# The first loads of a fused attention and MLP kernel: x's second tile on ACT's queue, b1 first on GpSimd's queue, b1's transpose behind those of the normalised rows

## The chip, the core and the metric

One NeuronCore of a Trainium2 chip runs the whole kernel. Its engines work side by side and meet through semaphores: PE (TensorE, the matrix unit, with its weight loads listed apart as PEld), DVE (VectorE), ACT (ScalarE), POOL (GpSimd) and SP (SyncE, here only an issuer of DMAs). SP, ACT and POOL each have a DMA queue of their own; in the profile these are q1 (SP), q10 (ACT) and q0 (POOL, called software_dynamic). An engine takes its instructions in the order in which they are written, and an instruction that waits holds up all behind it on that engine.

The metric is the device time of one launch in microseconds (us). The kernel before takes 795.08 us, the median of three runs (794.21 to 796.0).

## What is computed

Input x has 2048 rows of 512. Part A is a recurrent attention: the rows are cut into 64 segments of 32, each segment attends over 8 memory rows and itself with 32 heads of 128, and the first 8 output rows become the memory of the next segment. Part B is an MLP on every row. A gate mixes both:

```python
def _B_ref(x, w1, b1, w2, b2):
    y = _layernorm(x, axis=-1)
    h = _gelu(jnp.einsum('bsd,df->bsf', y, w1) + b1)      # 512 -> 1376
    return jnp.einsum('bsf,fd->bsd', h, w2) + b2          # 1376 -> 512
...
g = _sigmoid((x * gate_w).sum(-1, keepdims=True))
a = _A_ref(x, A_mem0, A_Wq, A_Wk, A_Wv, A_Wo, A_seg_len)
b = _B_ref(x, B_w1, B_b1, B_w2, B_b2)
return g * a + (1 - g) * b
```

All inputs are bf16.

## The kernel before, in words

The MLP runs first, over all rows, and leaves (1 − g) b in a DRAM buffer `c_dr`; meanwhile the attention's large weights come in. Then the 64 segments run one after another. The order on each engine is the order of the program text (a manual schedule). The change touches only the start, the part before and around the first MLP block.

The MLP works on 8 blocks of two tiles of 128 rows. For each block, `prep` normalises: per tile `bn_stats` and `bn_aggr` on DVE (L422, L423), then for both tiles together the inverse root (for block 0 a square root on ACT, L426, and a reciprocal on DVE), then the normalised rows `y` (L434). `prep_tr` turns a tile of y by four PE transposes (L441; each is a matmul with the identity) into the PSUM banks X1 or X2 and copies the result on DVE to `yT` (L442). `a_mm` multiplies one of 11 slices of 128 columns of w1 with yT, four matmuls of 256 columns (L462), alternately into the PSUM banks SbF and W, and ACT applies gelu with the bias `b1_sb` (L463) into `hTm`. `b_mm` multiplies hTm with w2, two matmuls of 512 columns (L468), two units behind `a_mm`. So the first three units of `a_mm` stand alone, and from then on units of both alternate.

The bias b1 has 1376 values and has to stand across partitions, one column of 128 for each slice. It is loaded as 11 rows of 128 into `b1r` (two DMAs, since the last row has only 96 values; a memset fills the rest), turned by one PE transpose into `b1p`, which lies in bank W (L498), and copied to `b1_sb` by DVE (L500).

The order before the first block is this. POOL: the memsets of `BO`, the making of the identity `ident`, the memset of b1r (L324), the load of the gate weights `gw_bc` (L336, a broadcast to 128 partitions), constants for the masks. SP's queue: x's tiles 0 and 1 (`ld_x`, L309), the first 3 of 11 slices of w1 (L322), b1's two pieces (L325, L326), x's tiles 2 and 3, w1's slices 3 to 6 (L334) and 7 to 10 (L335), the later part of w2 (L337, L338), b2, x's tiles 4 and 5. ACT's queue: w2's slices 0 to 2 and 3 to 5 (L331), then a first activation that loads ACT's table. PE: 28 warm-up matmuls on the identity (L496, into bank U3, their results unused), the transpose of b1, the eight transposes of y, then `a_mm` of block 0. DVE: `prep(0)`, the copy of b1, the two copies of yT, then `prep(1)`.

The lines that order this on PE and DVE:

```python
        for _ in range(NWARM):
            nc.tensor.matmul(U[3][:, 0:P], lhsT=ident[:], rhs=ident[:], start=True, stop=True, skip_group_check=True)
        b1p = W[:].bitcast(BF16)[:, 0:FC]
        nc.tensor.transpose(b1p, b1r[:], ident[:FC, :FC])
        prep(0)
        nc.vector.tensor_copy(out=b1_sb[:], in_=b1p)
        for tt in range(TB):
            prep_tr(0, tt)
```

Of the kernel before, what the change touches and what calls it, by code (L numbers as in the profile page):

```python
# [10 lines left out]
BF16 = mybir.dt.bfloat16  # L11
# [16 lines left out]
def kernel(ctx, tc, A_x, A_mem0, A_Wq, A_Wk, A_Wv, A_Wo, A_seg_len, B_x, B_w1, B_b1, B_w2, B_b2, gate_w, out):  # L28
    nc = tc.nc
    P = 128  # L30
# [6 lines left out]
    F = B_w1.shape[1]  # L37
# [3 lines left out]
    FC = (F + P - 1) // P  # L41
# [11 lines left out]
    x2 = A_x.rearrange("b s d -> (b s) d")  # L53
# [8 lines left out]
    ident = pers.tile([P, P], BF16)  # L62
# [6 lines left out]
    ep = early.enter_context(tc.tile_pool(name="ep", bufs=1))  # L69
# [9 lines left out]
    SelL = ep.tile([P, P], BF16)  # L79
    SelI = ep.tile([P, 32], BF16)  # L80

    nc.gpsimd.memset(BO[:], 0.0)
    for g in range(4):
        nc.gpsimd.memset(BO[32 * g:32 * g + 32, 32 * g:32 * g + 32], 1.0)
# [207 lines left out]
    with tc.tile_pool(name="mlpw", bufs=1) as mlpw, \  # L292
# [2 lines left out]
        TB = 2  # L295
        NBLK = NT // TB
        LAG = 2
        FR = F - (FC - 1) * P
        assert FR % 32 == 0 and FR < P
        w1_sb = mlpw.tile([P, KC, F], BF16)  # L300
        w2_sb = mlpw.tile([P, FC, Dm], BF16)
        b1_sb = mlpw.tile([P, FC], BF16)
# [1 line left out]
        hTm = [mlpw.tile([P, FC, TB * P], BF16, name=f"hTm{i}") for i in range(2)]  # L304
        xts = {}

        def ld_x(T):
            xt = mwork.tile([P, Dm], BF16, tag="xt", bufs=6, name="xt")
            nc.sync.dma_start(xt[:], x2[T * P:(T + 1) * P, :])  # L309
            xts[T] = xt  # L310

        def ld_w(W_, A, n):
# [4 lines left out]

        F0 = 3 * P
        ld_x(0)
        ld_x(1)  # L320
        w1v = B_w1.rearrange("(kc p) f -> p kc f", p=P)
        nc.sync.dma_start(w1_sb[:, :, 0:F0], w1v[:, :, 0:F0])  # L322
        b1r = mlpw.tile([FC, P], BF16)
        nc.gpsimd.memset(b1r[:], 0.0)  # L324
        nc.sync.dma_start(b1r[0:FC - 1, :], B_b1[0:(FC - 1) * P].rearrange("(c p) -> c p", p=P))  # L325
        nc.sync.dma_start(b1r[FC - 1:FC, 0:FR], B_b1[(FC - 1) * P:F].rearrange("(o p) -> o p", o=1))  # L326

        NWARM = 28
        H1, H2, F1 = 3, 6, 7 * P
        for a, b in ((0, H1), (H1, H2)):  # L330
            nc.scalar.dma_start(w2_sb[:, a:b, :], B_w2[a * P:b * P, :].rearrange("(fc p) d -> p fc d", p=P))  # L331
        ld_x(2)
        ld_x(3)
        nc.sync.dma_start(w1_sb[:, :, F0:F1], w1v[:, :, F0:F1])  # L334
        nc.sync.dma_start(w1_sb[:, :, F1:F], w1v[:, :, F1:F])  # L335
        nc.gpsimd.dma_start(gw_bc[:], gate_w.partition_broadcast(P))  # L336
        nc.sync.dma_start(w2_sb[:, H2:FC - 1, :], B_w2[H2 * P:(FC - 1) * P, :].rearrange("(fc p) d -> p fc d", p=P))  # L337
        nc.sync.dma_start(w2_sb[:FR, FC - 1, :], B_w2[(FC - 1) * P:F, :])  # L338
        nc.sync.dma_start(w2_sb[FR:FR + 1, FC - 1, :], B_b2.rearrange("(o d) -> o d", o=1))
        ld_x(4)  # L340
# [40 lines left out]
        def consts():  # L381
            nc.vector.tensor_scalar(out=rr[:, 0:1], in0=ri[:], scalar1=31, scalar2=None, op0=ALU.bitwise_and)
            nc.vector.tensor_scalar(out=rr[:, 2:3], in0=rr[:, 0:1], scalar1=2, scalar2=None, op0=ALU.logical_shift_right)
            nc.vector.tensor_scalar(out=rr[:, 1:2], in0=rr[:, 0:1], scalar1=3, scalar2=None, op0=ALU.bitwise_and)
            nc.vector.tensor_copy(out=rf[:], in_=rr[:])
            nc.vector.tensor_copy(out=iof[:], in_=io[:])
            nc.vector.tensor_scalar(out=rf[:, 0:1], in0=rf[:, 0:1], scalar1=float(M), scalar2=None, op0=ALU.subtract)
            nc.vector.tensor_scalar(out=mk1[:], in0=iof[:, 0:4], scalar1=rf[:, 1:2], scalar2=MASK_NEG, op0=ALU.not_equal, op1=ALU.mult)
            yield
            for a in range(4):  # L390
                nc.vector.tensor_scalar(out=Mk[:, a, 16:16 + RIDE], in0=iof[:], scalar1=rf[:, 0:1], scalar2=MASK_NEG, op0=ALU.is_lt, op1=ALU.mult)
                nc.vector.tensor_copy(out=Mk[:, a, 0:8], in_=mk1[:, a:a + 1].to_broadcast([P, 8]))
                nc.vector.tensor_scalar(out=Mk[:, a, 48:56], in0=iof[:, 0:8], scalar1=rf[:, 2:3], scalar2=MASK_NEG, op0=ALU.is_lt, op1=ALU.mult)
                nc.vector.tensor_scalar(out=Mk[:, a, 48:56], in0=Mk[:, a, 48:56], scalar1=mk1[:, a:a + 1], scalar2=None, op0=ALU.add)
                yield


        for i in range(2):
            nc.gpsimd.memset(hTm[i][FR:FR + 1, FC - 1, :], 1.0)
        z_all = mlpw.tile([P, NT], FP32)  # L400
# [15 lines left out]
        def prep(blk):  # L416
            mv = msmall.tile([P, TB, nc.vector.BN_AGGR_DIM], FP32, tag="mv", name="mv")
            ve = msmall.tile([P, TB], FP32, tag="ve", name="ve")
            rs = msmall.tile([P, TB], FP32, tag="rs", name="rs")
            for tt in range(TB):  # L420
                st = msmall.tile([P, nc.vector.BN_STATS_DIM], FP32, tag="st", name="st")
                nc.vector.bn_stats(out=st[:], in_=xts[blk * TB + tt][:])  # L422
                nc.vector.bn_aggr(out=mv[:, tt, :], in_=st[:])  # L423
            nc.vector.tensor_scalar(out=ve[:], in0=mv[:, :, 1], scalar1=LN_EPS, scalar2=None, op0=ALU.add)
            if blk == 0:
                nc.scalar.activation(out=rs[:], in_=ve[:], func=ACTF.Sqrt)  # L426
                nc.scalar.activation(out=dummy[:], in_=ident[:, 0:1], func=ACTF.Gelu_apprx_tanh)
                nc.vector.reciprocal(out=rs[:], in_=rs[:])
            else:
                rsqrt(rs[:], ve[:], TB)  # L430
            for tt in range(TB):
                T = blk * TB + tt
                ys[T] = mwork.tile([P, Dm], BF16, tag="y", name="y")
                nc.vector.tensor_scalar(out=ys[T][:], in0=xts[T][:], scalar1=mv[:, tt, 0:1], scalar2=rs[:, tt:tt + 1], op0=ALU.subtract, op1=ALU.mult)  # L434
            yTs[blk] = mwork.tile([P, KC, TB * P], BF16, tag="yT", name="yT")

        def prep_tr(blk, tt):
            y, bk = ys.pop(blk * TB + tt), (X1, X2)[tt]
            tp = bk[:].bitcast(BF16)[:, 0:Dm].rearrange("p (k t) -> p k t", k=KC)
            for kc in range(KC):  # L440
                nc.tensor.transpose(tp[:, kc, :], y[:, kc * P:(kc + 1) * P], ident[:])  # L441
            nc.vector.tensor_copy(out=yTs[blk][:, :, tt * P:(tt + 1) * P], in_=tp)  # L442
# [52 lines left out]
        for _ in range(NWARM):  # L495
            nc.tensor.matmul(U[3][:, 0:P], lhsT=ident[:], rhs=ident[:], start=True, stop=True, skip_group_check=True)  # L496
        b1p = W[:].bitcast(BF16)[:, 0:FC]
        nc.tensor.transpose(b1p, b1r[:], ident[:FC, :FC])  # L498
        prep(0)
        nc.vector.tensor_copy(out=b1_sb[:], in_=b1p)  # L500
        for tt in range(TB):
            prep_tr(0, tt)
        side0 = iter(())
        cgen = consts()
        units = [(blk, fc) for blk in range(NBLK) for fc in range(FC)]
# [133 lines left out]
    for s in range(nseg):  # L639
        T, si = divmod(s, SPT)  # L640
# [127 lines left out]
    o = cw.tile([P, Dm], BF16, tag="o", name="o")  # L768
# [125 lines left out]
```

## Time and profile before

| | |
|---|---|
| median of three runs | 795.08 us (794.21 to 796.0) |
| the profiled execution's own time | 796.19 us |
| its span on the core | 794.4 us |
| PE busy | 767.9 us, 97% of the span |
| ACT busy | 539.9 us, 68% |
| DVE busy | 327.7 us, 41% |
| POOL busy | 277.8 us, 35% |
| moved by DMA | 70.49 MB, mean 89 GB/s |
| first MLP matmul (L462) | 9.53 us after the span's start |

The profile is of one execution. Its page lists the busy time of each engine, the span in 40 slices, the chain of work that ended last followed back to the start, and groups of instructions by line. A row of the timeline has the start, the length, the engine, the line, the operation with its tile, and in brackets the idle time of the engine ahead of it and what ended that. A row of the chain of waits has the start, the length and what the end of the kernel hung on at that time. A row of a DMA queue has packets, MB and the share of 16 engines' time in the window; a row of DMA issues has KB for each and the median us from issue to landing. In the rows of a tile, names are shortened: `w_sb` stands for w1 and w2 both, `b_sb` for b1_sb, `xt` for all tiles of x. Matmuls are pipelined and their ends are modelled, so the distance between starts, or the chain's lengths, tell their rate better than the length of one.

### The profile page before, as it was taken

Reading aid. Unit: us, or ns where it says so; the run is one execution under the profiler, and the core shown is the slowest. Engines: PE = TensorE matmul, PEld = TensorE weight load, DVE = VectorE, ACT = ScalarE, POOL = GpSimd, SP = SyncE. Lnnn points to the kernel's source line nnn. Section 1 sums busy time; section 2 is a strip of 40 time slices with the busy share of each in tenths; the row PEclk is TensorE's granted clock in tenths of the full one; section 3 lists DMA queues with packets and bytes.
Section 4 is the critical chain, followed back from the end, with each engine's and each line's share of the span. In section 5 each row is a group of like instructions: output and inputs, shape, how many; then the busy total and the mean of one; then the engine's idle time right before and its main releaser. Section 6 shows DMA issues by size and latency. Waiting matters only on the chain.

```text
span 794.4 us, 42412 instructions
## 1 busy us (share of the span) xinstructions
PE 767.9 (97%) x18921; PEld 428.8 (54%) x18950; DVE 327.7 (41%) x1061; ACT 539.9 (68%) x1503; POOL 277.8 (35%) x519
## 2 busy tenths in 40 slices
PE   7999999999999999999999999999999999999996
PEld 5666555555555555555555555555555555555553
DVE  4776344333334343434343333434343434333334
ACT  3666676766777676767776677777677767776663
POOL 3111033343344434234334324443334434332332
PEclk9999999999999999999999999999999999999999
DMA  6779411212111222211121212122221212121211
GB/s 189 265 269 350 142 59 58 74 60 86 60 53 68 77 70 70 77 57 60 60 86 61 86 61 75 46 75 70 78 70 57 62 58 86 61 80 60 71 65 36
DMA packets 46723, 70.49 MB, mean 89 GB/s; under 512 B 12799, under 2 KB 36456, under 8 KB 45000
## 3 DMA queue, kind: packets, MB, share of 16 engines
q1 hardware_dynamic: 45016, 64.97, 25.0%
q8 instruction: 150, 2.46, 1.3%
q0 software_dynamic: 720, 1.97, 0.7%
q10 hardware_dynamic: 800, 0.79, 0.3%
q14 instruction: 37, 0.30, 0.1%
HBM read 59.06 MB, written 4.45 MB: 80 GB/s over the span
## 4 chain that ended last, share of the span: by engine, by line
PE 93%; ACT 4%; issue 1%; DVE 1%; DMA 1%; POOL 0%; SPq 0%; DVEq 0%; POOLq 0%; ACTq 0%
PE U L110 28%; PE X L129 18%; PE W L141 14%; PE X L110 7%; PE U L468 5%; PE U L280 4%; PE X L141 3%; ACT w L635 3%; PE W L462 3%; PE SbF L462 3%; PE W L724 2%; PE U L267 1%; PE SbF L605 1%; PE SbF L256 1%; PE W L248 1%
## 5 line engine op out<-in xcount | busy, mean ns | idle before, releaser
L629 POOL TENSOR_TENSOR UT<-XR,Rb 128x384 bf16<-128x384 bf16 x126 | 140.0, 1132 | 271.8 <-DMA Rb<-r_dr 211.7
L115 ACT CAST Tb<-U 128x512 bf16<-128x512 f32 x258 | 151.0, 585 | 83.2 <-PE U L110 82.7
L110 PEld LDWEIGHTS <-hT 128*32 128x32 bf16 x4096 | 103.9, 97 | 109.7 <-DVE hT L725 19.1
L110 PE MATMUL U<-Wq_sb,hT 128*32 128x512 bf16 x2048 | 132.8, 379 | 1.1 <-DVE hT L725 1.1
L129 PE MATMUL X<-Wv_sb,hT 128*32 128x512 bf16 x2048 | 133.2, 378 | 0.0
L110 PE MATMUL U<-Wk_sb,hT 128*32 128x512 bf16 x2048 | 132.7, 379 | 0.0
L141 PE MATMUL W<-Wo_sb,UT 128*32 128x512 bf16 x2080 | 124.6, 380 | 1.5 <-ACT UT L712 1.2
L725 DVE CAST hT<-W 128x32 bf16<-128x32 f32 x63 | 12.1, 192 | 231.2 <-PE W L724 231.2
L119 DVE STREAM_TRANSPOSE QT<-Tb 128x256 f32<-128x256 f32 x128 | 57.0, 445 | 82.2 <-ACT Tb L115 81.1
L141 PEld LDWEIGHTS <-UT 128*32 128x32 bf16 x2080 | 57.2, 96 | 58.0 <-POOL racc L621 19.0
L119 DVE STREAM_TRANSPOSE KT<-Tb 128x256 f32<-128x256 f32 x128 | 57.0, 445 | 58.2 <-ACT Tb L115 58.2
L611 ACT CAST XR<-U 128x256 bf16<-128x256 f32 x252 | 78.6, 438 | 0.0
L635 ACT CAST w<-W 128x512 bf16<-128x512 f32 x65 | 38.0, 585 | 45.2 <-PE W L141 45.2
L629 POOL TENSOR_TENSOR UL<-XR,Rb 128x128 bf16<-128x128 bf16 x126 | 60.4, 500 | 0.0
L712 ACT CAST UT<-U 128x64 bf16<-128x64 f32 x252 | 35.3, 227 | 31.3 <-PE U L285 31.3
L129 PEld LDWEIGHTS <-hT 128*32 128x32 bf16 x2048 | 45.2, 95 | 20.7
L681 DVE RECIPROCAL R<-U 128x32 f32<-128x32 f32 x126 | 45.0, 357 | 25.9 <-PE U L270 23.0
L621 POOL TENSOR_TENSOR racc<-racc,R 128x72 f32<-128x72 f32 x63 | 21.2, 336 | 97.9 <-DVE R L616 95.2
L468 PE MATMUL U<-w_sb,hTm 128*128 128x512 bf16 (+1 forms) x163 | 49.5, 381 | 0.6
L115 ACT CAST Tb<-X 128x512 bf16<-128x512 f32 x62 | 36.5, 589 | 16.4 <-PE X L110 16.4
L462 PEld LDWEIGHTS <-w_sb 128*128 128x128 bf16 (+1 forms) x352 | 34.7, 102 | 21.1 <-issue 4.0
L256 PEld LDWEIGHTS <-KT 128*32 128x32 bf16 x2048 | 33.7, 95 | 16.3 <-DVE KT L119 0.2
(158 smaller groups left out, 1176.0 us busy)
## 6 DMA issues: line engine op xcount, KB each, us to landing
Rb<-r_dr SPq DMA_DIRECT2D x63, 512.0 KB, 3.9
Wv_sb<-in_A_Wv_dram SPq DMA_DIRECT2D x4, 1024.0 KB, 7.0
Wq_sb<-in_A_Wq_dram SPq DMA_DIRECT2D x4, 1024.0 KB, 7.2
Wk_sb<-in_A_Wk_dram SPq DMA_DIRECT2D x4, 1024.0 KB, 10.7
Wo_sb<-in_A_Wo_dram SPq DMA_DIRECT2D x4, 1024.0 KB, 14.8
VP<-VL SPq DMA_DIRECT2D x64, 64.0 KB, 3.0
xt<-in_A_x_dram SPq DMA_DIRECT2D x16, 128.0 KB, 2.7
xs<-in_A_x_dram SPq DMA_DIRECT2D x16, 128.0 KB, 2.3
```

Of the source, the lines that this page charges most:

```text
L110: nc.tensor.matmul(bk[32 * j:32 * j + 32, :], lhsT=G[:, kc, :], rhs=W5[t][:, kc, h0:h1, j, :], start=(kc == 0), stop=(kc == KC - 1), tile_ ...
L115: nc.scalar.copy(out=Tb[:], in_=bk.rearrange("p (a b e) -> p a e b", a=8, b=2))
L119: nc.vector.transpose(out=dst[:, 8 * hf:8 * hf + 8, 0:32, :].rearrange("p a r b -> p a (r b)").bitcast(FP32), in_=Tb[:].rearrange("p a e b ...
L129: nc.tensor.matmul(bk[32 * j:32 * j + 32, :], lhsT=G[:, kc, :], rhs=Wv5[:, kc, 4 * vb:4 * vb + 4, j, :], start=(kc == 0), stop=(kc == KC - ...
L141: nc.tensor.matmul(bk[32 * c:32 * c + 32, :], lhsT=U_[:, j, i, :], rhs=Wo_sb[:, 4 * i + j, :], start=(n == 0), stop=(n == NW - 1), tile_po ...
L256: nc.tensor.matmul(Sb[i2][32 * j:32 * j + 32, i - 4 * i2, M:M + 40], lhsT=KT[:, h // 2, :, h % 2], rhs=QT[:, h // 2, :, h % 2], start=Fals ...
L462: nc.tensor.matmul(hp[:rows, 0:TB * P], lhsT=w1_sb[:, kc, fc * P:fc * P + rows], rhs=yTs[blk][:, kc, :], start=(kc == 0), stop=(kc == KC - 1))
L468: nc.tensor.matmul(bp(blk, tt)[:], lhsT=hTm[blk % 2][:rows, fc, tt * P:(tt + 1) * P], rhs=w2_sb[:rows, fc, :], start=(fc == 0), stop=(fc = ...
L611: nc.scalar.copy(out=XR[:, j], in_=U[j][:, 0:NG * 40].rearrange("p (i q) -> p i q", q=40)[:, :, 8:40])
L629: nc.gpsimd.tensor_tensor(out=out[:, :, 4 * h:4 * h + 4, o:o + b - a], in0=XR[:, :, 4 * h:4 * h + 4, a:b], in1=Rb[:, h, :, :, a:b], op=ALU ...
L635: nc.scalar.copy(out=w[:], in_=W[:])
L681: nc.vector.reciprocal(out=r, in_=U[i2][:, 320:352])
```

## The change

Three edits, all at the start.

1. `ld_x` takes the issuing engine as an argument, and tile 1 of x is issued by ACT, ahead of ACT's two pieces of w2.
2. b1r, its memset and its two loads move to the head of the kernel and to POOL: memset, then both loads on GpSimd's queue, ahead of the memsets of BO and the making of the identity. SP's queue has two DMAs fewer. b1r is now allocated from the pool `ep`, which lives longer than the MLP's pool.
3. On PE, b1's transpose comes behind the eight transposes of y, and on DVE its copy comes behind the two copies of yT.

```diff
+    b1r = ep.tile([FC, P], BF16)
+    FR = F - (FC - 1) * P
+    nc.gpsimd.memset(b1r[:], 0.0)
+    nc.gpsimd.dma_start(b1r[0:FC - 1, :], B_b1[0:(FC - 1) * P].rearrange("(c p) -> c p", p=P))
+    nc.gpsimd.dma_start(b1r[FC - 1:FC, 0:FR], B_b1[(FC - 1) * P:F].rearrange("(o p) -> o p", o=1))
     nc.gpsimd.memset(BO[:], 0.0)
     for g in range(4):
         nc.gpsimd.memset(BO[32 * g:32 * g + 32, 32 * g:32 * g + 32], 1.0)
...
-        def ld_x(T):
+        def ld_x(T, eng=nc.sync):
             xt = mwork.tile([P, Dm], BF16, tag="xt", bufs=6, name="xt")
-            nc.sync.dma_start(xt[:], x2[T * P:(T + 1) * P, :])
+            eng.dma_start(xt[:], x2[T * P:(T + 1) * P, :])
             xts[T] = xt
...
         ld_x(0)
-        ld_x(1)
+        ld_x(1, nc.scalar)
         w1v = B_w1.rearrange("(kc p) f -> p kc f", p=P)
         nc.sync.dma_start(w1_sb[:, :, 0:F0], w1v[:, :, 0:F0])
-        b1r = mlpw.tile([FC, P], BF16)
-        nc.gpsimd.memset(b1r[:], 0.0)
-        nc.sync.dma_start(b1r[0:FC - 1, :], B_b1[0:(FC - 1) * P].rearrange("(c p) -> c p", p=P))
-        nc.sync.dma_start(b1r[FC - 1:FC, 0:FR], B_b1[(FC - 1) * P:F].rearrange("(o p) -> o p", o=1))
...
         b1p = W[:].bitcast(BF16)[:, 0:FC]
-        nc.tensor.transpose(b1p, b1r[:], ident[:FC, :FC])
         prep(0)
-        nc.vector.tensor_copy(out=b1_sb[:], in_=b1p)
         for tt in range(TB):
             prep_tr(0, tt)
+        nc.tensor.transpose(b1p, b1r[:], ident[:FC, :FC])
+        nc.vector.tensor_copy(out=b1_sb[:], in_=b1p)
```

More of the change, by code (lines that the diff above doesn't have):

```diff
@@ L297 @@
         LAG = 2
-        FR = F - (FC - 1) * P
         assert FR % 32 == 0 and FR < P
```

## The prediction

> **What bounds the kernel now.** First the page: shares of the engines, then the chain of waits.
>
> ```profile
> PE 767.9 (97%) x18921; PEld 428.8 (54%) x18950; DVE 327.7 (41%) x1061; ACT 539.9 (68%) x1503; POOL 277.8 (35%) x519
> PE 93%; ACT 4%; issue 1%; DVE 1%; DMA 1%; POOL 0%; SPq 0%; DVEq 0%; POOLq 0%; ACTq 0%
> ```
>
> TensorE is the bound of the whole span. The change touches only what comes before the MLP's steady rhythm, so the question is how much earlier that rhythm starts; whatever PE gains there it keeps, since 93% of the chain behind it is PE's own work. The chain in order of time, first 15 us:
>
> ```profile
> 2.68 5.06 DMA b1r<-in_B_b_dram
> ...
> 7.88 0.16 PE W L498
> 8.04 0.55 PE X L441 x4
> ...
> 8.62 0.42 DVE yT L442
> ...
> 9.05 0.43 DVE yT L442
> ...
> 9.53 1.01 PE SbF L462 x4
> 10.54 0.85 PE W L462 x4
> 11.39 0.87 PE SbF L462 x4
> ...
> 12.89 0.96 PE W L462 x4
> 13.85 0.43 PE U L468 x2
> 14.28 0.44 PE SbF L462 x4
> ```
>
> Two things stand there. The chain runs through the landing of b1's second piece, because its transpose (L498) stands ahead of y's transposes (L441) in PE's order. And a group of four L462 matmuls takes 0.85 to 0.87 us until 12.3, but 0.44 from 14.28: PE runs at half rate at first. The page's clock row shows full clock throughout, so durations alone tell it. The timeline shows the same stretch by engine:
>
> ```profile
> 0.76 0.87 SPq L309 DMA_DIRECT2D xt<-in_A_x_dram  x2
> 1.79 1.28 ACT L493 ACT_TABLE_LOAD   x1 [1.79 <-issue]
> 1.94 0.19 POOL L324 MEMSET b1r<- 11x128 bf16 x1
> 2.04 3.17 PE L496 MATMUL U<-ident 128*128 128x128 bf16 x28 [2.04 <-POOL ident masks.py:199]
> 2.08 0.73 POOL L336 DMA_DIRECT2D gw_bc<-in_gate_w_dram  x1
> 3.55 0.69 DVE L422 BATCH_NORM_STATS2 st<-xt 128x6 f32<-128x512 bf16 x1 [3.55 <-DMA xt<-in_A_x_dram]
> 5.04 0.69 DVE L422 BATCH_NORM_STATS2 st<-xt 128x6 f32<-128x512 bf16 x1 [0.59 <-DMA xt<-in_A_x_dram]
> 6.69 0.73 DVE L434 TENSOR_SCALAR y<-xt,mv,rs 128x512 bf16<-128x512 bf16 x2
> 7.88 0.16 PE L498 MATMUL W<-ident,b1r 11*128 11x11 bf16 x1 [2.67 <-DMA b1r<-in_B_b_dram]
> 7.98 1.03 PE L441 MATMUL X<-ident,y 128*128 128x128 bf16 x8
> ```
>
> The first y is ready at about 7.1 (half of the 0.73 behind 6.69), but PE stands until 7.88 for b1: 2.67 us idle. Half rate holds through the warm-up (28 in 3.17, 0.11 each), through that gap, and for 4.1 us of unbroken work from 9.53 to about 13.6 (late in the group that starts at 12.89; the pair of L468 behind it has the full rate, 0.43).
>
> **Part 1, x's second tile on ACT's queue.** Order of the packets before, by queue (q1 is SP's, q10 ACT's), in the windows 1.5 to 3 us, 3 to 4, and 4 to 4.5:
>
> ```profile
> q1 hardware_dynamic: 134, 0.13, 56.3%
> ...
> q10 hardware_dynamic: 373, 0.37, 104.7%
> q1 hardware_dynamic: 21, 0.02, 4.9%
> ...
> q1 hardware_dynamic: 133, 0.12, 69.1%
> q10 hardware_dynamic: 73, 0.07, 39.7%
> ```
>
> The second tile (128 packets) does not follow the first on SP's queue: ACT's first piece of w2 (384 packets) goes in between, and x comes at 4 to 4.5. At the head of ACT's queue it takes that turn instead: at 373 packets per us its 128 are through by about 3.35, and seen some 0.55 later (the first tile's packets end at 3.0 and DVE starts at 3.55), at 3.9. DVE isn't free for it until 3.55 + 0.69 + 0.13 = 4.37 (in a later pair of tiles the second statistics start 0.82 behind the first: 9.39 and 10.21, below). So 5.04 becomes 4.37, and the first y is ready at 7.1 − 0.67 = 6.4.
>
> ```profile
> 9.39 0.68 DVE L422 BATCH_NORM_STATS2 st<-xt 128x6 f32<-128x512 bf16 x1
> ...
> 10.21 0.66 DVE L422 BATCH_NORM_STATS2 st<-xt 128x6 f32<-128x512 bf16 x1
> ```
>
> [...]
>
> What ACT issues behind it, w2's two pieces, moves back by one issue (0.43) and one turn of 128 packets; the first L468 needs them only behind three groups of L462. ACT's table load moves from 1.79 to 2.2 and ends at 3.5, ahead of the second statistics that its square root waits for. SP's pieces behind x move up.
>
> **Part 2, b1 first of all on GpSimd.** One memset (0.19) is only moved. Two DMA issues are new on POOL, and POOL holds up behind each. The trace has prices:
>
> ```profile
> 6.25 0.55 POOL L399 MEMSET hTm<- 1x256 bf16 x2
> ...
> L478 POOL DMA_DIRECT2D c_dr<-ct x14: 539/539/563, 23.5 to 85.0; - x14
> ```
>
> One at 0.73 (as gw_bc, the first on that queue) and one at 0.54, with 0.19 and gaps: 1.5 us (bounds 1.3 and 1.7) ahead of the memsets of BO and the making of ident. The warm-up waits for ident: 2.04 becomes 3.55, its end 5.1 becomes 6.6. This was covered by PE's idle time; now it is not quite: it is the last thing that y's transposes wait for (6.6 against y's 6.4), so each 0.1 more on POOL costs 0.1. POOL's later work (constants, the memset of hTm at 6.25, gw_bc) moves back about as much; hTm's first write is a gelu at about 8.8.
>
> When does b1 land? No small load on POOL's queue is in the trace; the rows nearest are:
>
> ```profile
> gw_bc<-in_gate_w_dram POOLq DMA_DIRECT2D x1, 128.0 KB, 5.9
> ...
> c_dr<-ct POOLq DMA_DIRECT2D x2, 128.0 KB, 7.3
> ...
> c_dr<-ct POOLq DMA_DIRECT2D x2, 128.0 KB, 4.2
> ```
>
> Second piece issued at 1.7: landing at 7.6 by the load of the same stretch, which I take; 5.9 and 9.0 are the ends.
>
> **Part 3, b1's transpose behind y's.** y's eight transposes start at 6.6 instead of 7.98 and end at about 7.5. b1's (0.16) then waits for the landing at 7.6, and its copy (0.17) on DVE comes behind yT's two. PE would idle there anyway for yT: first transpose to first L462 is 9.53 − 7.98 = 1.55, so L462 starts at 8.2. A landing up to about 7.9 is free; behind it wait all of PE's L462 and, through them, the gelus, one for one: at 9.0 L462 starts at 9.3. **Start: 9.53 becomes 8.2, 1.3 us.**
>
> **The slow stretch.** With the warm-up at 3.55 to 6.6 and y's transposes behind it at once, PE works unbroken for 3.9 us to 7.5, then with a gap of 0.7. Before, 3.0 us and a gap of 2.7 did not bring the full rate, 4.1 us did. I take the full rate from about 8 on, that is for all of L462 (the other bound: counting starts anew at 8.2, full rate at 12.3). Then three groups at 0.44 end at 9.5, the pair of L468 (0.43) at 9.95, and the fourth group needs w1's second piece:
>
> ```profile
> 5.06 0.43 SPq L334 DMA_DIRECT2D w_sb<-in_B_w_dram  x1
> ...
> w_sb<-in_B_w_dram SPq DMA_DIRECT2D x1, 512.0 KB, 5.2
> ```
>
> It lands at 10.26. Its issue moves up, but the bytes ahead of it stay nearly the same, so I keep 10.26. The fourth group and its pair (0.44 + 0.43) end at 11.13, where now it is 14.12. **Sum: 14.12 − 11.13 = 3.0 us**, 1.3 of it shift, some 2.0 rate, less 0.3 waited for w1. Nothing later takes it back: the window 14.12 to 16.72 below moves no byte, so all that block 0 reads is in.
>
> ```profile
> 14.12:16.72 2.60, 2.60 (x19) 1.76 (x18) 0.10 (x1) 1.41 (x4) 0.00 (x0) 1.00 0.00 0
> ```
>
> The profiled execution took 796.19 (span 794.4 and 1.79 around it): 793.2. It lies 1.11 above the median of the three runs (795.08; 794.21 to 796.0). Whatever of the 1.11 is a long slow stretch goes with the change, the rest is the profiled run's own; between 795.08 − 3.0 = 792.1 and 793.2 I take **792.7**.
>
> [...]
>
> **Rivals.**
> - *Shift without rate* (chance 0.16): the gap at 7.5 counts, the full rate comes 4.1 us after 8.2, at the same place in the work. Gain 1.3: 793.8 from the median. For it: the warm-up and its gap did nothing before. Against: that gap was 2.7, this one 0.7.
> - *The rate changes at its own time* (0.06): at 13.6 whatever PE did. Work brought forward by 1.3 at half rate is worth 0.7: 794.4. Against: three runs spread over 1.8 us.
> - *b1 a little late* (0.12): landing 8.0 to 9.2 as the row of 7.3 allows. At 9.0 L462 starts at 9.3; with full rate the fourth group's pair ends near 11.9 (gain 2.2, 792.9), without it the gain is 0.2 (794.9).
> - *b1 late on the software queue, slower* (0.14): queues take turns of about 1 us, as the counts of 3 to 4 us show, and b1's two pieces may each lose one. 1.7 + 7.3 + 2 is a landing at 11.0; L462 starts at 11.3, 1.8 later than now, PE has idled 3.5 us ahead of it and the slow stretch starts anew: 795.08 + 1.8 = 796.9. It decides from a landing at 9.3 on, where L462 starts no earlier than now; each us behind that costs one. Against it, packets of POOL's queue q0 between 6.5 and 7 us (gw_bc's, issued at 2.08):
>
> ```profile
> q0 software_dynamic: 37, 0.13, 98.8%
> ```
>
> Nearly all 128 KB moved within 5 us of the issue, in the busiest stretch.
> - *Hidden anyway* (0.04): w1's second piece lands later by what the start wins: no change, 795.1.
>
> **Numbers.** The forecast has 0.48. A measurement of this kernel tells from about 0.2% (1.6 us). Faster: 0.46 of the forecast, 0.07 of the shift alone (it lies 0.3 us short of the bound), 0.09 of b1 a little late, **0.62**. Within: 0.02, 0.09, all of the rate at its own time (0.06), 0.03 of b1 a little late, 0.02 of the software queue, 0.02 hidden, **0.24**. Slower: 0.12 of the software queue, 0.02 hidden and worse, **0.14**. Range **791.2 to 795.4**: down to the sum without the wait for w1 and with the whole 3.3 taken from the median (791.8), less what runs spread; up past the cases without a gain (795.1). Left out is most of the slower case. The forecast's own range is 791.8 to 793.4.
>
> **What would show it.** Second statistics at about 4.4 without a DMA wait; warm-up at 3.5; y's transposes at 6.6; L498 behind them with a wait under 0.5; first L462 at 8.2, groups of 0.44 from there; a wait of PE near 10 for w1. Wrong if L498 waits for b1 past 8, if L462's groups still take 0.86, or if x's second tile lands after 4.4.

## The result, and the profile after

| | median of 22 runs | lowest to highest |
|---|---|---|
| before | 795.54 us | 794.21 to 796.48 |
| changed | 793.71 us | 792.95 to 794.87 |

The ratio is 0.9979, with a 95% interval of 0.9972 to 0.9985: the change makes the kernel about 1.7 us faster, a fifth of a per cent (the medians lie 1.83 us apart). All times here were measured at a granted clock of 0.99 or more, but for one run of the experiment sp44w (969.08 us at 0.752), which its ratio leaves out. The forecast was 792.7 us from 795.08, a ratio of 0.9970; the direction and the range held, the gain came out a quarter to a third smaller.

The profiled execution of the changed kernel took 793.25 us, its span 791.4. PE is still the bound:

```profile
PE 768.7 (97%) x18950; PEld 427.9 (54%) x18950; DVE 327.8 (41%) x1061; ACT 539.8 (68%) x1503; POOL 279.1 (35%) x521
```

The chain of waits of the changed kernel, at its start (start, length, what the end hung on; the transpose of b1 is now L501, b1's loads L85 and L86):

```profile
0.75 0.19 POOL b1r L84
...
1.35 0.70 POOL b1r L85
2.05 0.54 POOL b1r L86
...
3.46 0.20 POOL gw_bc L336
...
4.07 0.32 POOL ident masks.py:199
...
4.43 3.17 PE U L496 x28
7.60 0.44 PE X L441 x4
...
8.07 0.76 DVE yT L442 x2
...
9.51 0.48 ACT hTm L463
...
10.04 0.60 PE SbF L462 x4
```

Before, this chain began on GpSimd too, but then went through a DMA, b1's landing. Now it stays on GpSimd up to the identity and goes on through the warm-up: GpSimd has taken the DMA's place. The timeline of the changed kernel by engine:

```profile
4.47 0.66 DVE L422 BATCH_NORM_STATS2 st<-xt 128x6 f32<-128x512 bf16 x1
6.05 0.82 DVE L434 TENSOR_SCALAR y<-xt,mv,rs 128x512 bf16<-128x512 bf16 x2
7.40 0.86 PE L441 MATMUL X<-ident,y 128*128 128x128 bf16 x8
8.19 0.18 PE L501 MATMUL W<-ident,b1r 11*128 11x11 bf16 x1
8.88 0.60 PE L462 MATMUL SbF<-yT,w_sb 128*128 128x256 bf16 x4 [0.51 <-DVE yT L442]
...
11.77 0.60 PE L462 MATMUL SbF<-yT,w_sb 128*128 128x256 bf16 x4
```

The second statistics start at 4.47 with no wait for a DMA, the first y is ready at about 6.5, and then it lies still for almost a microsecond until the warm-up lets PE go. The first L462 starts 0.65 us earlier than before (8.88 against 9.53), the fifth group of L462, where both kernels run in their steady rhythm, 2.35 us earlier (11.77 against 14.12): shift and rate, as the forecast split them. The groups run at full rate from the first on (a row of four has a length of 0.60; before, 1.01 at first). The two profiles lie 2.94 us apart, more than the medians, for two reasons: the profiled execution of before was one of the slower ones (796.19), that of the changed kernel one of the faster; and some 0.8 us of it arises far behind the change. The last operation on DVE, before and after:

```profile
788.89 0.75 DVE L769 SCALAR_TENSOR_TENSOR o<-X,g_all,c 128x512 bf16<-128x512 f32 x1 [0.87 <-PE X L766]
```

```profile
785.78 0.75 DVE L769 SCALAR_TENSOR_TENSOR o<-X,g_all,c 128x512 bf16<-128x512 f32 x1 [0.87 <-PE X L766]
```

The distance has grown from 2.35 to 3.11 on the way, in a part of the program that the change doesn't touch. What lengthens a segment here and there in one execution and not in the other was not looked into; no number below rests on it.

### The profile page after: what moved, and what is told of

It is laid out like the page before. It is cut to its first block, busy times and chain, and to the rows that moved or that the text cites. A ratio compares the mean times of both kernels' runs of the same rounds, so it can differ in the third digit from the quotient of the medians.

```text
span 791.4 us, 42443 instructions
## 1 busy us (share of the span) xinstructions
PE 768.7 (97%) x18950; PEld 427.9 (54%) x18950; DVE 327.8 (41%) x1061; ACT 539.8 (68%) x1503; POOL 279.1 (35%) x521
## 4 chain that ended last, share of the span: by engine, by line
PE 93%; ACT 3%; DVE 1%; issue 1%; POOL 0%; DVEq 0%; POOLq 0%
PE U L115 28%; PE X L134 18%; PE W L146 14%; PE X L115 7%; PE U L468 5%; PE U L285 4%; PE X L146 3%; ACT w L635 3%; PE W L462 2%; PE SbF L462 2%; PE W L724 1%; PE U L272 1%; PE SbF L605 1%; PE SbF L261 1%; PE W L253 1%
## 5 line engine op out<-in xcount | busy, mean ns | idle before, releaser
L468 PE MATMUL U<-w_sb,hTm 128*128 128x512 bf16 (+1 forms) x176 | 52.0, 379 | 0.0
L462 PEld LDWEIGHTS <-w_sb 128*128 128x128 bf16 (+1 forms) x352 | 34.0, 100 | 20.2 <-issue 3.5
```

Source lines behind the costliest of these rows:

```text
L462: nc.tensor.matmul(hp[:rows, 0:TB * P], lhsT=w1_sb[:, kc, fc * P:fc * P + rows], rhs=yTs[blk][:, kc, :], start=(kc == 0), stop=(kc == KC - 1))
L468: nc.tensor.matmul(bp(blk, tt)[:], lhsT=hTm[blk % 2][:rows, fc, tt * P:(tt + 1) * P], rhs=w2_sb[:rows, fc, :], start=(fc == 0), stop=(fc = ...
```

## The experiments

The theory on record: the gain is part shift, part rate, and the changed kernel's start hangs on where the warm-up stands. The rivals: the shift alone, x's early tile alone, or the order on PE alone. Twelve kernels, each timed in five rounds (6 to 12 runs) beside the kernel before, on three chips. The ratios are those on record; the quotients of the medians differ from them by up to 0.0006. "First" and "fifth" are the starts of the first and fifth group of L462 in the kernel's one profile, "full clock" the time from which that profile's trace records PE's granted clock as full.

| kernel | first | fifth | full clock | ratio to before (95%) |
|---|---|---|---|---|
| before | 9.53 | 14.12 | 13.62 | 1 |
| changed | 8.88 | 11.77 | 7.90 | 0.9979 (0.9972 to 0.9985) |
| x_only | 10.55 | 14.46 | 13.24 | 0.9994 (0.9985 to 1.0002) |
| b1_only | 9.15 | 12.49 | 8.32 | 0.9984 (0.9975 to 0.9993) |
| tr_only | 8.64 | 12.35 | 10.92 | 0.9987 (0.9978 to 0.9995) |
| warm56 | 9.35 | 12.24 | 7.29 | 0.9973 (0.9962 to 0.9984) |
| id_mid | 8.02 | 11.55 | 7.01 | 0.9970 (0.9959 to 0.9981) |
| id_mid_gw | 7.92 | 10.81 | 6.91 | 0.9953 (0.9940 to 0.9966) |
| tr44_gw | 8.54 | 11.43 | 5.32 | 0.9965 (0.9952 to 0.9977) |
| after0 | 8.28 | 12.27 | 11.15 | 0.9981 (0.9970 to 0.9991) |
| id_first | 8.21 | 12.50 | 5.37, half from 8.79 to 12.20 | 0.9979 (0.9969 to 0.9988) |
| sp28 | 10.03 | 14.66 | 14.18 | 1.0010 (1.0001 to 1.0019) |
| sp44 | 9.80 | 14.30 | 7.43, half from 10.84 to 14.26 | 0.9996 (0.9986 to 1.0006) |
| sp44w | 9.76 | 14.14 | 7.15, half from 10.57 to 13.98 | 1.0004 (0.9992 to 1.0015) |

The last column but one settles what the durations only suggest; before's 13.62 is the prediction's 13.6. (The views of the profile count the time ahead of the first such record as full clock, so the clock row could not show the slow stretch.) The time differs from profile to profile, also behind the same warm-up: where 28 matmuls ran from 2.04 or 2.05 for 3.17 us, the clock was full from 10.92 (tr_only), 13.24 (x_only), 13.62 (before) and 14.18 (sp28). Nor did it always last: it went back to half in id_first at 8.79, behind waits of PE of 1.83 and 0.89 us, in sp44 at 10.84, behind one of 2.02, and in sp44w at 10.57, behind one of 2.11; in tr44_gw it stayed full through waits of 1.07 and 0.41. What sets these times is not shown, and when the clock became full in the runs without a profile is not known.

### The three parts, each alone

**x_only**, the kernel before with

```diff
-        ld_x(1)
+        ld_x(1, nc.scalar)
```

> Part 1 alone (x's second tile on ACT's queue). Theory (the gain is the place of the warm-up and the order on PE): second statistics at about 4.5 and the first y at 6.5, but PE still waits for b1, which moves up with SP's queue by one issue (0.43) at most. L498 at 7.3 to 7.9, first L462 at 9.0 to 9.5, its groups at half rate until past 13: 0 to 0.4 us faster than before. Rival (x's early tile is what brings the gain): first L462 near 8.2 and 1.3 us or more faster.

```profile
8.90 0.17 PE L498 MATMUL W<-ident,b1r 11*128 11x11 bf16 x1 [3.69 <-DMA b1r<-in_B_b_dram]
...
10.55 1.01 PE L462 MATMUL SbF<-yT,w_sb 128*128 128x256 bf16 x4 [0.52 <-DVE yT L442]
```

No gain in time, as expected, but the profile isn't as expected: b1 was to come up to 0.4 us earlier and came 1.0 later (8.90 against 7.88). From 6 to 7 us SP's queue moved only 11 packets here, while ACT's queue moved 161 (0.15 MB) and gw_bc's load 0.11 MB; no run separates the two. x's early tile by itself brings nothing.

**b1_only**, the loads and the memset of b1 moved to GpSimd as in the change, the rest as before.

> Part 2 alone (b1 first on GpSimd's queue, its transpose still ahead of y's). Theory: ident at about 4.4 as in the changed kernel, warm-up to 7.5, b1 lands at about 7.6, first L462 at 9.3 to 9.5, so hardly a shift; but the late warm-up brings the full rate before the first L462: the groups take 0.44 and the fifth group starts near 12.2 instead of 14.1: 1.3 to 1.9 us faster. Rival (the rate does not depend on where the warm-up stands): 0 to 0.2 us faster, groups of 0.86 for 4 us.

```profile
4.44 3.17 PE L496 MATMUL U<-ident 128*128 128x128 bf16 x28 [4.44 <-POOL ident masks.py:199]
7.60 0.16 PE L498 MATMUL W<-ident,b1r 11*128 11x11 bf16 x1
...
9.15 0.60 PE L462 MATMUL SbF<-yT,w_sb 128*128 128x256 bf16 x4 [0.56 <-DVE yT L442]
...
11.61 0.61 PE L462 MATMUL W<-yT,w_sb 128*128 128x256 bf16 x4 [0.49 <-DMA w_sb<-in_B_w_dram]
```

The first group starts only 0.4 us earlier, its row has a length of 0.60, that of full rate, where before has 1.01, and the time falls by 0.16%, the lower end of the expectation. That is the rate almost by itself: the warm-up ends right where PE's work begins, and the clock is full from 8.32. The wait of 0.49 for w1's second piece, which the prediction had foreseen for the changed kernel, shows here.

**tr_only**, b1's transpose and copy behind y's, nothing else:

```diff
-        nc.tensor.transpose(b1p, b1r[:], ident[:FC, :FC])
         prep(0)
-        nc.vector.tensor_copy(out=b1_sb[:], in_=b1p)
         for tt in range(TB):
             prep_tr(0, tt)
+        nc.tensor.transpose(b1p, b1r[:], ident[:FC, :FC])
+        nc.vector.tensor_copy(out=b1_sb[:], in_=b1p)
```

> Part 3 alone (b1's transpose and copy behind y's). Theory: y's transposes start at 7.1 to 7.2, b1 has landed at 7.75 and costs nothing, first L462 at 8.7 at half rate, the slow stretch ends at 12.8 to 13.6: 0.4 to 0.9 us faster. Rival (the order on PE alone brings most of the 1.7 us): 1.4 us or more.

```profile
8.64 1.01 PE L462 MATMUL SbF<-yT,w_sb 128*128 128x256 bf16 x4 [0.40 <-DVE yT L442]
```

A shift of 0.9 as expected. The slow stretch ended at 10.92 in this execution, earlier than expected; the time fell by 0.13%. By the ratios the order on PE gives more than half of what the whole change gives, with no move between queues; the intervals overlap. The three single gains add to 0.35%, the change has 0.21%. That shift and rate shorten the same half-rate work would explain a smaller whole, but with some 0.08% of uncertainty on each the difference isn't shown.

### The rate by itself

**warm56**, the kernel before with twice the warm-up:

```diff
-        NWARM = 28
+        NWARM = 56
```

> The kernel before with 56 warm-up matmuls instead of 28 and nothing else. Theory: the warm-up runs from 2.04 to between 6.7 and 8.0 and closes PE's gap, so PE is at full rate at the first L462, which starts at 9.2 to 9.7; groups of 0.44, fifth group near 12.4: 1.2 to 1.8 us faster. Rival (the gain is the shift alone): 0 to 0.2 us slower, and groups of 0.86.

```profile
2.05 5.78 PE L496 MATMUL U<-ident 128*128 128x128 bf16 x56 [2.05 <-POOL ident masks.py:199]
8.01 0.16 PE L498 MATMUL W<-ident,b1r 11*128 11x11 bf16 x1 [0.18 <-DMA b1r<-in_B_b_dram]
...
9.35 0.60 PE L462 MATMUL SbF<-yT,w_sb 128*128 128x256 bf16 x4 [0.62 <-DVE yT L442]
```

One number changed, and the gain is 0.27%, as much as that of the whole change (0.21%, the intervals overlap). PE's wait for b1 (2.67 us before) is filled with matmuls whose results nobody uses; 0.18 is left of it, and all of block 0 runs at full rate. By the medians the gain is 1.84 us, the upper end of the expectation. The seven runs lie between 793.92 and 794.59, where thirty of before on the same chip spread from 794.49 to 798.10. In the profile PE works from 2.05 to 7.83 without a gap in the row, and the clock is full from 7.29, 2.06 us ahead of the first L462; that this narrows the spread is the author's guess, not shown.

**after0**, the changed kernel with `NWARM = 0`:

> The changed kernel without any warm-up matmul. Theory (the late warm-up holds the start back by some 0.8 us but pays for it with the full rate): y's transposes at 6.5, first L462 at 7.9 to 8.2 unless b1 (7.6) is later, groups of 0.86 until 10.5 to 13: 0.4 to 1.2 us slower than the changed kernel, ratio 0.9985 to 0.9995. Rival (the shift alone makes the gain): 0.7 us faster than the changed kernel, ratio 0.9970.

```profile
6.73 1.04 PE L441 MATMUL X<-ident,y 128*128 128x128 bf16 x8 [6.73 <-POOL SelI L376]
...
8.28 1.01 PE L462 MATMUL SbF<-yT,w_sb 128*128 128x256 bf16 x4 [0.33 <-DVE yT L442]
```

0.9981, between the two expectations and not to be told from the changed kernel's 0.9979. In the profile the mechanism is as stated: the first group is 0.6 earlier than with the warm-up, the rate is half until 11.15, and the fifth is 0.5 later. So in the profiles the late warm-up of the changed kernel costs 0.6 in shift of the 1.1 that it brings in rate; in the times no difference is to be seen.

### What holds the changed kernel's start

**id_mid**, the changed kernel with `make_identity` written between b1's loads and BO's memsets:

```diff
+    make_identity(nc, ident[:])
     nc.gpsimd.memset(BO[:], 0.0)
...
-    make_identity(nc, ident[:])
```

> The changed kernel with the identity written ahead of BO's memsets, so that on GpSimd its last step comes right behind b1's two loads, and BO's memsets and gw_bc's load behind it. Theory (the identity's lateness on GpSimd holds the whole start of the changed kernel): warm-up from about 3.1 instead of 4.43, y's transposes at 6.5, first L462 at 8.0 to 8.3 instead of 8.88, then perhaps a wait for w1's second piece near 10.6: 0.3 to 0.7 us faster than the changed kernel, ratio 0.9970 to 0.9975. Rival (y or b1 is what the start waits for): first L462 at 8.8 and 0.9979. Second rival (a warm-up that ends earlier leaves the rate low): groups of 0.86 and slower than the changed kernel.

```profile
3.04 3.17 PE L496 MATMUL U<-ident 128*128 128x128 bf16 x28 [3.04 <-POOL ident masks.py:199]
6.60 0.79 PE L441 MATMUL X<-ident,y 128*128 128x128 bf16 x8 [0.39 <-DVE y L434]
...
8.02 0.60 PE L462 MATMUL SbF<-yT,w_sb 128*128 128x256 bf16 x4 [0.48 <-DVE yT L442]
...
10.68 0.61 PE L462 MATMUL W<-yT,w_sb 128*128 128x256 bf16 x4 [0.47 <-DMA w_sb<-in_B_w_dram]
```

All of it as expected: warm-up at 3.04, first group at 8.02, a wait for w1's second piece until 10.68, and 0.9970. By its interval the time alone can't be told from the changed kernel's 0.9979; the starts in the profile can. The identity's lateness on GpSimd is what the start of the changed kernel waits for; once it is gone, PE waits for y (0.39) and then for w1.

**id_first**, the identity ahead of b1's memset and loads as well:

> The changed kernel with the identity made first of all on GpSimd, b1's two loads behind it. Theory (where the warm-up ends matters more than when it begins): warm-up from 1.7 to 4.9, b1's second piece issued near 2.7 and landed at 8.2 to 8.5, first L462 at 8.5 to 9.0 at half rate: 0.5 to 1.2 us slower than the changed kernel, ratio 0.9986 to 0.9994. Rival (an early identity is all that the changed kernel lacks): as with the identity behind b1's loads, 0.9970.

```profile
1.48 3.17 PE L496 MATMUL U<-ident 128*128 128x128 bf16 x28 [1.48 <-POOL ident masks.py:199]
6.48 0.75 PE L441 MATMUL X<-ident,y 128*128 128x128 bf16 x8 [1.83 <-DVE y L434]
8.11 0.16 PE L501 MATMUL W<-ident,b1r 11*128 11x11 bf16 x1 [0.89 <-DMA b1r<-in_B_b_dram]
8.21 0.61 PE L462 MATMUL SbF<-yT,w_sb 128*128 128x256 bf16 x4
8.66 0.92 PE L462 MATMUL W<-yT,w_sb 128*128 128x256 bf16 x4
```

```profile
5.38:8.78 3.40, 1.42 (x15) 1.06 (x16) 2.33 (x8) 1.69 (x3) 2.86 (x16) 1.00 1.04 280
8.79:12.20 3.41, 3.41 (x16) 2.04 (x14) 2.96 (x15) 1.45 (x4) 0.00 (x0) 0.50 1.08 364
```

The last two lines are stretches of time: start and end, length, the busy time of PE, PEld, DVE, ACT and POOL, then the granted clock. 0.9979, as the changed kernel: the expected loss did not show in the time, and its interval reaches to the rival's 0.9970. The profile decides against the rival: the warm-up has gaps of 1.83 and 0.89 us behind it, and the full rate that PE had at 8.21 is lost at 8.79, in the second group; from 5.38 to 8.78 PE was busy for only 1.42 of 3.40 us. The warm-up had not been too short: its 28 matmuls ended at 4.65, the clock was full at 5.37, ahead of any other work of PE (6.48), and it was lost behind the gaps. The first group starts about when it does in id_mid (8.21 against 8.02), the fifth 0.95 us later (12.50 against 11.55).

### The other queue for b1, which failed

**sp28**: x's second tile on ACT's queue and the new order on PE as in the change, GpSimd as before, and b1 on SP's queue behind x's first tile, with its memset on DVE.

```diff
         ld_x(0)
+        b1r = mlpw.tile([FC, P], BF16)
+        nc.vector.memset(b1r[:], 0.0)
+        nc.sync.dma_start(b1r[0:FC - 1, :], ...)
+        nc.sync.dma_start(b1r[FC - 1:FC, 0:FR], ...)
         ld_x(1, nc.scalar)
```

> x's second tile on ACT's queue, b1's two loads on SP's queue right behind x's first tile (its memset on DVE), b1's transpose behind y's; GpSimd as before, so the identity at 2.0 and 28 warm-up matmuls that end at 5.2. Theory (shift and rate are separate, and the rate needs a warm-up that reaches up to the work): y's transposes at 6.5, first L462 at 7.9 to 8.1, a shift of 1.5, but at half rate for 2 to 4 us: 1.0 to 1.6 us faster than before, about as the changed kernel. Rival (the rate comes with the transposes anyway): 2.4 us or more.

```profile
10.03 1.03 PE L462 MATMUL SbF<-yT,w_sb 128*128 128x256 bf16 x4 [2.51 <-DMA w_sb<-in_B_w_dram]
```

Missed, and slower than before by a tenth of a per cent. y's transposes did run at 6.36, but then PE stood 2.51 us for w1's first piece, which nothing had waited for until then. The packets from 3.5 to 5 us in this kernel (q10 is ACT's queue, q1 SP's):

```profile
q10 hardware_dynamic: 506, 0.50, 97.9%
q1 hardware_dynamic: 22, 0.02, 4.7%
```

Behind two loads of 2.7 KB together, SP's queue moves next to nothing while ACT's queue has the engines. That w1's piece was issued behind both of ACT's pieces here (1.94) would explain this as well as a turn that each small load costs its queue; no run tells them apart. It is only part of the delay, too: from 5 to 8 us gw_bc's load, issued at 1.94 here, holds 28.4, 51.8 and 29.8% of the engines' time in one us each, and SP's queue moves 0.13, 0.07 and 0.15 MB, against 0.34 from 8 to 9. sp28 with gw_bc's load late was not run, so the share of each in the 2.51 us is open.

**sp44** is sp28 with 44 warm-up matmuls.

> As the one with b1 on SP's queue, with 44 warm-up matmuls instead of 28. Theory: warm-up from 2.04 to about 6.4, full rate from the first L462 at 7.9 to 8.1 on; the fourth group waits for w1's second piece to about 10.3: fifth group at 11.2 or a little later, 2.2 to 2.8 us faster than before (ratio 0.9965 to 0.9972). Rival (no more than the change itself is to be had): 0.9979.

```profile
9.80 0.61 PE L462 MATMUL SbF<-yT,w_sb 128*128 128x256 bf16 x4 [2.02 <-DMA w_sb<-in_B_w_dram]
...
10.98 1.01 PE L462 MATMUL SbF<-yT,w_sb 128*128 128x256 bf16 x4
```

Missed for the same reason, w1's first piece. It shows one thing more: PE had the full rate at 9.80 and lost it at 10.84, behind the wait of 2.02 us.

**sp44w** is sp44 with w1's second piece ahead of x's third and fourth tiles.

> As the one with 44 warm-up matmuls, with w1's second piece ahead of x's third and fourth tiles on SP's queue. Theory (w1's second piece is the next bound): its wait is gone, the fourth group starts at 9.9 and the fifth at 10.8: 0.2 to 0.5 us faster than with 44 alone. Rival (x's third tile comes late and the second block's y with it): no gain or a wait of PE for y near 15.

Undecided: with the first piece late, the second is not what PE waits for. The ratio is 1.0004.

### One that beats the change, and one at least as good

**id_mid_gw**, id_mid with the load of gw_bc, which is read only at 16 us, behind the constants and memsets on GpSimd:

```diff
-        nc.gpsimd.dma_start(gw_bc[:], gate_w.partition_broadcast(P))
...
         for i in range(2):
             nc.gpsimd.memset(hTm[i][FR:FR + 1, FC - 1, :], 1.0)
+        nc.gpsimd.dma_start(gw_bc[:], gate_w.partition_broadcast(P))
```

> The kernel with the identity right behind b1's loads, with gw_bc's load issued behind the constants and memsets on GpSimd instead of at 3.1. Theory (gw_bc's few long packets hold the DMA engines for about 1 us ahead of w1's second piece): that piece lands at 9.7 to 10.1 instead of 10.68, PE's wait for it is gone or under 0.1: 0.3 to 0.5 us faster than without this, ratio 0.9963 to 0.9967. Rival (the bytes ahead of it alone set when it lands): under 0.2 us.

Packets from 6 to 9 us, first in id_mid, then in id_mid_gw:

```profile
q1 hardware_dynamic: 492, 0.47, 49.9%
q0 software_dynamic: 75, 0.13, 34.0%
```

```profile
q1 hardware_dynamic: 862, 0.83, 86.3%
...
q0 software_dynamic: 32, 0.00, 0.7%
```

```profile
9.94 0.60 PE L462 MATMUL W<-yT,w_sb 128*128 128x256 bf16 x4
```

gw_bc's 0.13 MB holds the 16 engines for a third of these 3 us; without it SP's queue moves 0.83 MB in the same time instead of 0.47. The fourth group starts at 9.94 with no wait for w1 (10.68 in id_mid), because that piece landed 6.8 us after its issue instead of 7.8. The kernel's ratio is 0.9953, with medians of 792.40 us against 795.73 on the same chip (3.33 us, or 0.42%). That is more than was expected (0.9963 to 0.9967, inside its interval), and in six runs the best of all: about twice what the change gains.

**tr44_gw**, the kernel before with the order of tr_only, `NWARM = 44` and gw_bc's load late as above, and no move between queues.

> The kernel before with three small edits and no move between queues: b1's transpose behind y's, 44 warm-up matmuls, gw_bc's load behind the constants on GpSimd. Theory: warm-up to 6.9, y's transposes at 7.1, first L462 at 8.3 to 8.6 at full rate, no wait for w1's second piece: fifth group near 11.2, 2.2 to 2.8 us faster than before, ratio 0.9964 to 0.9972, so better than the change. Rival (x's second tile and b1 have to move queues for more than 1.7 us): 0.9979 or worse.

```profile
8.54 0.60 PE L462 MATMUL SbF<-yT,w_sb 128*128 128x256 bf16 x4 [0.41 <-DVE yT L442]
```

0.9965, as expected; its interval overlaps the change's a little. Against it, what is left for the earlier x and for b1 on GpSimd is the 0.12% up to id_mid_gw, and the two intervals overlap.

## Why the prediction was right, and what was mis-sized

- **The bound and the mechanism** held. b1's landing ahead of y's transposes was the wait, and half rate was the larger part: b1_only has the rate with a small shift, tr_only a shift at half rate (until 10.92), warm56 the rate with no edit but a number.
- **Part 1** held in its times: second statistics at 4.47 for 4.37 (the first were 0.10 later too), y at about 6.5 for 6.4; had the second tile come earlier by its issue alone (0.43, half of the 0.87 for two on SP), the statistics would have started at 4.6. That whole pieces take turns, or queues for about 1 us, isn't shown by them: here the two tiles moved side by side (57 packets of SP's queue and 76 of ACT's from 1.5 to 2.5 us), and in the kernel before the order of issue gives the same order of pieces as turns do.
- **Part 2 was mis-sized**, and this is the term that failed. "1.5 us ahead of the memsets of BO and the making of ident" took the two issues and the memset, and nothing else to change on POOL. The issues cost what the rows said (0.70 and 0.55). But the warm-up came 2.39 later than before (4.43 for 2.04), outside the bounds of 1.3 and 1.7. The last step of ident came behind BO's memsets before, too. New are 0.26 us in which POOL stands ahead of the first issue, and gw_bc's issue (0.57, and 0.10 behind it), which the text has far later. Before, then changed:

```profile
1.03 0.58 POOL L84 MEMSET BO<- 32x32 bf16 x4
...
1.70 0.29 POOL masks.py:199 TENSOR_SCALAR_AFFINE_SELECT ident<-ident 128x128 bf16<-128x128 bf16 x1
```

```profile
1.35 0.70 POOL L85 DMA_DIRECT2D b1r<-in_B_b_dram  x1 [0.26 <-POOL BO L87]
...
3.40 0.57 POOL L336 DMA_DIRECT2D gw_bc<-in_gate_w_dram  x1
4.07 0.31 POOL masks.py:199 TENSOR_SCALAR_AFFINE_SELECT ident<-ident 128x128 bf16<-128x128 bf16 x1
```

  Before the hand-ordered part of the program, the order on POOL isn't the text's (in the kernel before, the identity's memset at 0.89 stood between BO's memsets), and the new instructions changed it. "Each 0.1 more on POOL costs 0.1" was nearly right: 0.88 more than assumed put y's transposes at 7.40 for 6.6 and the first L462 at 8.88 for 8.2. id_mid, where the warm-up starts at 3.04, gives 0.9970, the forecast's own ratio; that the figures agree is in part chance, since its interval takes in the change's 0.9979.
- **b1's landing** was taken as 7.6 from gw_bc's row. It was 2.04 + 5.6 = 7.64, by luck: the issue came 0.34 later than assumed, and the load took 0.3 less. The rows for L85 and L86 in the changed kernel:

```profile
b1r<-in_B_b_dram POOLq DMA_DIRECT2D x1, 2.5 KB, 5.1
b1r<-in_B_b_dram POOLq DMA_DIRECT2D x1, 0.2 KB, 5.6
```

  So the rivals of a late b1, the slower one too, did not come about; L501 did not wait. Where PE was ready sooner, it did wait for b1: 0.89 in id_first (second piece issued at 2.2), 0.47 in id_mid_gw.
- **The slow stretch**: full rate at the first L462, as taken (recorded from 7.90), but the ground given, that 3.0 us of warm-up are too short and 4.1 us of work enough, isn't borne out. The same 28 matmuls (3.17 us) were followed by the full clock at 5.37 in id_first, where they ran from 1.48, and only at 13.62 in the kernel before, where they ran from 2.04. In the changed kernel PE was busy throughout from 4.43, the start of the warm-up, to 7.90 (3.47 us); in the kernel before it was busy for 3.17 us from 2.04 to 5.21, for 1.14 of 4.32 up to 9.53, and for 3.87 of 4.09 up to 13.62. What decides is not shown. Since behind the warm-up of before the full clock came at 10.92 in one kernel and at 14.18 in another, it may be in part luck that in this profile all of L462 had it. Not foreseen: at full rate the third group has to wait until the gelu of the first has emptied bank SbF (0.48 from 9.51, then 10.04); half rate had hidden that. It costs 0.3, as much as the forecast wait for w1's second piece, which did not show because the fourth group came later (the piece landed 7.8 us after its issue at 2.80, near 10.6, and the group started at 10.90); so the two errors cancel.
- **The sum**: 3.0 in the trace was 2.35, and the 0.65 between them is Part 2. By the medians it is 1.83. The changed kernel's profile had its full rate from 7.90 and that of before from 13.62, where tr_only, with the same warm-up as before, had it from 10.92; so the two may show more than the usual gain, and by how much can't be told from one profile of each. The step from 796.19 to the median was allowed for, about rightly: the median of before over 22 runs is 0.65 under its profiled run.
- **Shift without rate** and **the rate at its own time** are ruled out for the profiled executions; that the changed kernel gets the full rate as early in all of its 22 runs isn't shown, and its 1.9 us of spread, wider than the 0.7 of warm56, is a hint against it.

## What to carry to other kernels

The wait at the start was worth less here than the rate at which PE came out of it (0.65 us of the 2.35 by which the fifth group came earlier): before moving loads between queues, fill the wait with matmuls up to the first real one, which here took one number and gave as much as the whole change (0.27% against 0.21%). A warm-up that stops short of the work succeeded or failed here: 28 matmuls were followed by the full clock at 5.37 in id_first, lost again at 8.79, and only at 13.62 in the kernel before. When a DMA issue is put ahead on an engine, read off the new profile what that engine now does in which order, and put what the critical engine waits for (here the identity) ahead of what nobody needs yet. Look at what stands ahead of a load that the critical engine needs soon, and send late what is read late: with gw_bc's 128 KB sent late, w1's second piece landed 6.8 us after its issue instead of 7.8 (id_mid_gw, id_mid).

## Not expected of the hardware

- With two loads of 2.7 KB together ahead of it on SP's queue, w1's first piece kept PE waiting for 2.51 us, until 10.03 (sp28); between 3.5 and 5 us SP's queue moved 22 packets, ACT's 506. How much of it is the small loads' and how much gw_bc's is open.
- A load of 128 KB on GpSimd's queue held w1's second piece back by 1.0 us (landing 7.8 us after its issue in id_mid, 6.8 in id_mid_gw); it had 34.0% of the DMA engines' time from 6 to 9 us.
- PE's clock, once full, went back to half at 8.79 in id_first, at 10.84 in sp44 and at 10.57 in sp44w, behind waits of PE of 1.83 and 0.89 us, 2.02 and 2.11; in tr44_gw it stayed full through waits of 1.07 and 0.41. The same 28 warm-up matmuls, with no other work of PE behind them, were followed by the full clock at 5.37 in id_first; in the kernel before it came at 13.62.
